# Attention with normalised queries and keys: a warm-up add on GpSimd, another order of the first rows, and last stores behind the join of two branches

## The chip, the cores and the metric

The kernel runs on one core of one Trainium2 chip. Five engines work side by side and meet only through semaphores: TensorE (PE, with its weight loads shown apart as PEld), VectorE (DVE), ScalarE (ACT), GpSimd (POOL) and SyncE (SP), which here only starts transfers. The metric is the device time of one execution in microseconds; less is better. Before the change three executions gave 593.93, 594.44 and 594.76 us, so the median is 594.44 us.

## The reference: what is computed

```python
B, H, S, D = 1, 32, 2048, 640
Dh = D // H                      # 20
# q, k, v: [1, 32, 2048, 20] bfloat16, t: [32] bfloat16
def reference(q, k, v, t):
    eps = 1e-6
    qn = q / (jnp.sqrt((q * q).sum(axis=-1, keepdims=True)) + eps)
    kn = k / (jnp.sqrt((k * k).sum(axis=-1, keepdims=True)) + eps)
    logits = jnp.einsum('bhqd,bhkd->bhqk', qn, kn) * t[None, :, None, None]
    attn = _softmax(logits, axis=-1)
    return jnp.einsum('bhqk,bhkd->bhqd', attn, v)
```

There are 32 heads of 2048 x 2048 logits, with only 20 numbers per row of q and k. The dear part is therefore the exponential of 134 million logits, not the products.

## The kernel before

**Tiling.** Four heads are one group, so there are eight groups; 512 query columns of a group are one block, so there are 32 blocks. In a block each head has 16 key rows of 128 keys. One head's one key row against 512 queries is a unit: 2048 units in all. A unit's logits come from one product of PE (`psA<-qT,kT` or `psD<-qT,kT`, 128 x 512), and the four heads sit in four 32-row strips of PE, since `qpad` and `kpad` hold 20 numbers and 12 zeros for each head.

**Two ways to the exponential.** Two units at a time go through PSUM tile `psA` (two slots) and one ACTIVATE of 128 x 1024 on ACT into `pA`: call this a pair. The other units, taken four heads at a time, go one by one through `psD`: DVE makes an int16 line `dI` of them (a line that, read as float16, is a coarse power of two), and POOL adds a constant to the line twice (`int64_add`, four int16 at once) to give two shifted lines `dS`. These are called D units here. Their sum over four products with `vaug` or `vhalf` is a better exponential than any one of them. So a unit of a pair costs PE one product with v, a D unit four. All products with v add up in one bank of `psD`, with a column of ones in `vaug` giving the softmax's denominator.

**Start.** PE multiplies zeros (`zt`) as a warm-up; `HEAT0` is the count of these. DVE builds the identity `idn`; the first four rows of q and k of group 0 are loaded, squared, summed, rooted on ACT (`nrm`), scaled into `qpad` and `kpad`, turned by PE against `idn` and copied to `qT` and `kT`. The other twelve rows are done on DVE next, k and q, and turned by transposing transfers, except k's rows 4 to 7, which PE turns. POOL fills zeros and makes a band matrix `ind` with two AFFINE_SELECTs.

**The order is planned in Python.** `make_plan` plays the whole kernel through with a cost for each instruction and notes the order for each engine; the chip then runs these orders with semaphore waits. Constants such as `D_FROM` (the share of a block's pairs after which D units may begin), the overhead of a DVE instruction, or `ORDER` (a string that picks one of 23 sets of rules for each stretch of ten pairs) change the order and nothing else. So a small edit to them moves thousands of instructions.

**Two plans.** A flag from t (`flag`, the largest absolute t) picks at run time between a plan that uses D units and one that does not. Every engine loads the flag and branches; each engine's whole program past the first few instructions lies inside the branch's first arm, and the second arm follows it in the program. With the inputs here the first arm runs.

**End.** Each block is drained from `psD` by a transpose on DVE, inverted, and multiplied (`rec`, `omul`) into `ost`. The last block's result leaves in two transfers of 64 partitions, one from SP and one from ACT. They stand as the last instructions of the first arm; then each engine leaves the arm, SP waits for the transfers' landing, and all engines meet in a closing barrier.

The names that the steps below use: `first rows` are in `prep_ops` (called with rows 0 to 4), PE's turning in the loop that fills `pe_pre`, the copies in `copy`, POOL's start in `pool_init`, `sels` and `zeros`, the end in `issue` and `run`.

## Time and profile before

| what | value |
|---|---|
| median of three executions | 594.44 us |
| profiled execution, its own time | 594.49 us |
| span of the profiled execution (first to last instruction) | 592.7 us |
| PE, DVE, ACT, POOL busy | 581.3, 574.6, 580.4, 500.9 us |
| exponentials of 128 x 1024 on ACT | 628 |
| D units (lines `dI` of 128 x 512) | 792 |
| granted TensorE clock, mean | 0.998 |

The busy time of PE counts modelled ends of matmuls that overlap, so it is no sign that PE is full. Busy times of DVE and ACT are reliable as durations from start to written result, but two instructions that follow each other overlap by some ten nanoseconds: the distance from start to start is the better price. A row of the timeline gives start, length, engine, line and operation, the tile that is written and the one that is read, the count of merged instructions, and in brackets the idle time ahead of it and who ended that.

### The profile page before, as it was taken

The numbers are of one execution on the slowest core, as the hardware profiler recorded it, in microseconds if no ns is written. First come the engines' busy times: TensorE is split into PE (matmuls) and PEld (weight loads), VectorE is DVE, ScalarE is ACT, GpSimd is POOL, SyncE is SP. The second block draws the span as 40 slices with busy tenths as digits, with TensorE's granted clock in tenths as the row PEclk, the third lists the DMA queues.
The fourth block names the chain that finished last, engine by engine and source line by source line (L and its number), as shares of the span: only waits on it lengthen the run. The fifth ranks groups of instructions, "written<-read, shape, count | busy, mean of one in ns | idle before, by whom it ended". The sixth has DMA issues, their size and how long they took to land.

```text
span 592.7 us, 16383 instructions
## 1 busy us (share of the span) xinstructions
PE 581.3 (98%) x6768; PEld 160.2 (27%) x6768; DVE 574.6 (97%) x1016; ACT 580.4 (98%) x636; POOL 500.9 (84%) x951
## 2 busy tenths in 40 slices
PE   8999999999999999999999999999999999999996
PEld 4432222322223222232223222222222232222221
DVE  7999999999999999999999999999999999999993
ACT  6999999999999999999999999999999999999995
POOL 2488899878988799887998889987999978999994
PEclk9999999999999999999999999999999999999999
DMA  8700405205051131504033005330406104010000
GB/s 116 108 2 14 104 2 45 47 8 110 3 59 32 31 86 13 79 1 101 19 22 71 1 19 100 24 69 10 92 2 76 32 2 72 2 25 4 7 11 11
DMA packets 132145, 24.20 MB, mean 41 GB/s; under 512 B 121312, under 2 KB 132064, under 8 KB 132064
## 3 DMA queue, kind: packets, MB, share of 16 engines
q1 hardware_dynamic: 131264, 22.96, 24.6%
q8 instruction: 55, 0.90, 0.6%
q14 instruction: 26, 0.21, 0.1%
q10 hardware_dynamic: 800, 0.12, 0.1%
HBM read 7.87 MB, written 2.62 MB: 18 GB/s over the span
## 4 chain that ended last, share of the span: by engine, by line
ACT 87%; PE 10%; DVE 2%; POOL 1%; issue 0%
ACT pA L995 87%; PE psD L815 4%; PE psA L793 3%; PE psA L616 1%; PE psD L612 1%; POOL dS L374 1%; DVE dI L361 0%; PE psD L793 0%; PE psD L749 0%; DVE ssum L294 0%; DVE accT L386 0%; DVE sqs L291 0%; DVE kpad L338 0%; PE psD L616 0%; DVE ost L401 0%
## 5 line engine op out<-in xcount | busy, mean ns | idle before, releaser
L995 ACT ACTIVATE pA<-psA 128x1024 f16<-128x1024 f32 (+1 forms) x628 | 576.2, 1201 | 0.5 <-PE psD L793 0.2
L374 POOL INT64_ADD dS<-dI x935 | 494.5, 545 | 71.3 <-DVE ost L401 14.3
L361 DVE TENSOR_SCALAR dI<-psD 128x512 int16<-128x512 f32 (+1 forms) x768 | 488.1, 695 | 4.3 <-PE psD L793 2.5
L793 PE MATMUL psA<-qT,kT 32*128 32x512 bf16 x1256 | 246.4, 384 | 3.7 <-ACT pA L995 1.0
L793 PE MATMUL psD<-qT,kT 32*128 32x512 bf16 x795 | 237.6, 383 | 0.1
L815 PE MATMUL psD<-dS,vaug 128*22 128x512 f16 x1584 | 201.2, 383 | 0.1
L815 PE MATMUL psD<-pA,vaug 128*22 128x512 f16 (+1 forms) x1256 | 181.1, 383 | 0.3 <-POOL dS L374 0.3
L815 PE MATMUL psD<-dI,vaug 128*22 128x512 f16 x792 | 133.9, 383 | 0.0
L815 PE MATMUL psD<-dI,vhalf 128*22 128x512 f16 x792 | 131.4, 383 | 0.0
L793 PEld LDWEIGHTS psA<-qT,kT 32*128 32x128 bf16 x1256 | 59.0, 90 | 241.1 <-ACT pA L995 235.5
L793 PEld LDWEIGHTS psD<-qT,kT 32*128 32x128 bf16 x795 | 57.3, 91 | 11.1 <-DVE dI L361 4.8
L815 PEld LDWEIGHTS psD<-dS,vaug 128*22 128x22 bf16 x1584 | 42.9, 89 | 58.2 <-issue 38.2
L815 PEld LDWEIGHTS psD<-pA,vaug 128*22 128x22 bf16 x1256 | 39.6, 89 | 49.6 <-issue 41.2
L815 PEld LDWEIGHTS psD<-dI,vhalf 128*22 128x22 bf16 x792 | 29.7, 89 | 27.4 <-issue 20.0
L815 PEld LDWEIGHTS psD<-dI,vaug 128*22 128x22 bf16 x792 | 30.3, 89 | 23.4 <-issue 16.7
L386 DVE STREAM_TRANSPOSE accT<-psD 128x512 f32<-128x512 f32 x32 | 22.6, 705 | 4.6 <-PE psD L815 4.6
L401 DVE TENSOR_TENSOR ost<-accT,rec 128x320 bf16<-128x320 f32 x32 | 17.0, 532 | 0.1
L264 DVE TENSOR_TENSOR sqs<-qk 128x1280 bf16<-128x1280 bf16 x14 | 11.7, 835 | 0.0
L749 PE MATMUL psD<-ind,sqT 128*128 128x128 bf16 x140 | 11.3, 220 | 0.0
L612 PE MATMUL psD<-zt 128*128 128x128 bf16 x123 | 10.3, 221 | 0.0
L749 PEld LDWEIGHTS psD<-ind,sqT 128*128 128x128 bf16 x140 | 7.9, 98 | 4.5 <-issue 3.6
L612 PEld LDWEIGHTS psD<-zt 128*128 128x128 bf16 x123 | 7.0, 98 | 4.9 <-issue 4.9
(59 smaller groups left out, 84.7 us busy)
## 6 DMA issues: line engine op xcount, KB each, us to landing
vaug<-in_v_dram SPq DMA_DIRECT2D x32, 80.0 KB, 4.3
qk<-in_k_dram SPq DMA_DIRECT2D x7, 320.0 KB, 4.0
out_dram<-ost SPq DMA_DIRECT2D x28, 80.0 KB, 1.9
qk<-in_q_dram SPq DMA_DIRECT2D x6, 320.0 KB, 4.3
qk<-in_q_dram SPq DMA_DIRECT2D x4, 80.0 KB, 3.0
out_dram<-ost SPq DMA_DIRECT2D x7, 40.0 KB, 2.1
qk<-in_k_dram SPq DMA_DIRECT2D x1, 240.0 KB, 3.7
qk<-in_q_dram SPq DMA_DIRECT2D x1, 240.0 KB, 4.3
```

What stands on the lines that cost most here:

```text
L264: ops.append(dve("sq", w_, R2, lambda e, o=sq, x=x3: e.tensor_tensor(o, x, x, ALU.mult), [("qk", b, a, i) for i in parts] + [("qkx", b, i) ...
L361: lambda e: e.tensor_scalar(dst, psD[:, pb * QW:(pb + n) * QW], 1024.0 * LOG2E, 15360.0 - 1024.0 * LOG2K + SHIFTS[0], ALU.mult, ALU.add),
L374: lambda e: e.int64_add(o.bitcast(U64), x.bitcast(U64), add), rd, wr)
L386: return dve("drain", QW, R1, lambda e: e.transpose(accT[:, 16 * b:16 * b + 16, :].rearrange("p b d -> p (b d)"), psO_(sb)), [("psD", OB(s ...
L401: dve("omul", 320 * n, R1, lambda e: e.tensor_tensor(dst, num, rcb, ALU.mult), at + ar, [("ost", hg % 2, g) for g in range(g0, g1)]),
L612: return lambda e: e.matmul(bank, zt[:, 0:128], zt[:, 0:n], start=False, stop=False, skip_group_check=True)
L616: o.info = [lambda e: e.matmul(psO[:, :], zt[:, 0:128], zt[:, :])] + [(lambda e, i=i: e.matmul(psA[:, (i % 3) * QW:(i % 3 + 1) * QW], zt[: ...
L749: mms = [lambda e, g=g, j=j: e.matmul(dst, sqT[:, (5 * g + j) * 128:(5 * g + j + 1) * 128], ind[:, j, 96 - 32 * g:224 - 32 * g], start=g + ...
L793: return lambda e: e.matmul(dst, lhsT, rhs, tile_position=(32 * hh, 0))
L815: return lambda e: e.matmul(dst, lhsT, rhs, start=first, stop=last, skip_group_check=True, tile_position=(0, 32 * hh))
L995: a = Op("ACT", "exp", lambda e, s=src, d=dst: e.activation(d, s, ACT.Exp), [("psA", slot)], [("pA", pslot, i) for i in range(WAVES[slot]) ...
```

## The change

1. **GpSimd.** The two AFFINE_SELECTs no longer wait for `kpad`; after them POOL adds zero to a tile of 128 x 4 int16 (`tn`) once with `int64_add`. The zeroing for group 1's tiles moves behind some shifted lines.
2. **First rows.** `first_ops` takes q's and k's first four rows through separate squares, sums, roots and inverses; q is padded first, and k in two halves of two rows. PE's warm-up goes from 18 to 11 products, PE turns q ahead of k, and 3, 3 and 6 short zero products stand between. The copies are shared out anew.
3. **k's rest ahead of q's.** q's twelve remaining rows start only when k's inverse is there (squares) and when k's padded rows are there (sums). `D_FROM` goes from 0.12 to 0.07.
4. **Last stores.** The two last transfers stand behind the join of the two arms. They wait for a semaphore `fin_sem` of their own, which the last `omul` raises.
5. **The plan's numbers.** The overhead that the plan gives a DVE instruction goes from 0.069 to 0.065, a start is noted to the exact time, some other costs change, and `ORDER` is a new string.

```diff
-ORDER = "01i6e8h7238em08g57h5hi2i0gi1j2i0lgea8aa50a567i6538abh965h237050"
+ORDER = "90mfi9dkeb9bb210d6iccig0hgmg2k9baihi0il2h8cjmddh7egj8h9gghegjgc"
-D_FROM = 0.12
+D_FROM = 0.07
-HEAT0 = 18
+HEAT0 = 11
+WARM = (3, 3, 6)
+CPQ = ("DVE", "ACT")
-ACT0 = .0633
+ACT0 = .0634
-TRK = 1.2
+TRK = 0.0
-LOAD1 = 0
+LOAD1 = .12
...
-            o = Op("DVE", name, emit, reads, writes, cost=0.069 + c + ncols_fix,
+            o = Op("DVE", name, emit, reads, writes, cost=0.065 + c + ncols_fix,
...
+        def first_ops():
+            sqf, redf, nrmf, epsf, invf, scf = [], [], [], [], [], []
+            T_ = lambda tl, a: tl[:, a, :, 0:4]
+            for a, pad, nm in ((0, qpad, "qpad"), (1, kpad, "kpad")):
...
+                for c0, c1 in ((0, 4),) if a == 0 else ((0, 2), (2, 4)):
...
+            return sqf + redf + nrmf + [epsf[0]] + invf[0:2] + [scf[0], epsf[1], invf[2]] + scf[1:]
...
-            for o in sels:
+            tune = lambda e: e.int64_add(tn[:, :].bitcast(U64), zt[:, 0:4].bitcast(U64), 0)
+            for o in sels + [Op("POOL", "tune", tune, ["zt", "ind"], ["tn"], 6.0, 6.1)]:
                 o.alone = True
-                o.reads.append(("kpad", 0, 0))
                 want_dve(o, 1)
...
+            pe_pre.extend([warm(WARM[0]), turn("q", 0, 4, [psO, psO, psQ, psQ], [("psD", OB(0)), ("psD", 1)]), warm(WARM[1]),
+                           turn("k", 0, 2, [psD] * 2, [("psD", 0)]), warm(WARM[2])])
+            pe_mid = [turn("k", 2, 4, [psK] * 2, [("psD", 2)])]
...
-            copy("ACT", kT, psD, 0, 128, [("psD", 0)], kk[:1])
-            copy("DVE", qT, psO, 0, 256, [("psD", OB(0))], qq[:2])
-            copy("ACT", qT, psQ, 256, 512, [("psD", 1)], qq[2:])
-            copy("ACT", kT, psD, 128, 512, [("psD", 0)], kk[1:])
+            copy(CPQ[0], qT, psO, 0, 256, [("psD", OB(0))], qq[:2])
+            copy(CPQ[1], qT, psQ, 256, 512, [("psD", 1)], qq[2:])
+            copy("ACT", kT, psD, 0, 256, [("psD", 0)], kk[:2])
+            copy("DVE", kT, psK, 256, 512, [("psD", 2)], kk[2:])
...
                     if o.name == "sq":
-                        o.reads.append(gate)
-                    want_dve(o, 1.5)
+                        o.reads.append(("qT", 0, 1) if a0 else ("rn", 0, (4, 1, 2), 1))
+                    if o.name == "red" and not a0:
+                        o.reads.append(("kpad", 0, R - 1))
+                    want_dve(o, .8 if a0 else .9)
...
+                            if o.name == "omul" and cur == NSB - 1:
+                                o.sem, o.val = fin_sem, 1
...
+                if o.name == "out" and o.sem in ends:
+                    assert o is P.order[e][-1] and [d.sem for d in o.deps] == [fin_sem]
+                    continue
...
                 issue(eng, e, plans[1], cut[e], None)
+            if e == "SP":
+                for x in plans[0][0].order["SP"]:
+                    if x.name == "out" and x.sem not in ends:
+                        eng.wait_ge(x.sem, 16)
+            for o in plans[0][0].order[e][-1:]:
+                if o.name == "out":
+                    eng.wait_ge(fin_sem, 1)
+                    o.emit(eng).then_inc(o.sem, 16)
```

What the edits do to the order of the instructions is seen at three places. The first is PE's start, before (`psA<-zt` of 128 x 512 is the warm-up, `psD<-idn,...` the turning, `psA<-qT,kT` the first logits):

```order
L616 MATMUL psD<-zt 128x512
L616 MATMUL psA<-zt 128x512 x17
L1432 TENSOR_LOAD tmx
L1432 ISA x2
L1433 COMPARE_AND_BRANCH
L624 MATMUL psD<-idn,kpad 128x128 x4
L624 MATMUL psD<-idn,qpad 128x128 x4
L793 MATMUL psA<-qT,kT 128x512 x4
```

and now:

```order
L657 MATMUL psD<-zt 128x512
L657 MATMUL psA<-zt 128x512 x10
L1481 TENSOR_LOAD tmx
L1481 ISA x2
L1482 COMPARE_AND_BRANCH
L675 MATMUL psA<-zt 128x128 x3
L668 MATMUL psD<-idn,qpad 128x128 x4
L675 MATMUL psA<-zt 128x128 x3
L668 MATMUL psD<-idn,kpad 128x128 x2
L675 MATMUL psA<-zt 128x128 x6
L668 MATMUL psD<-idn,kpad 128x128 x2
L840 MATMUL psA<-qT,kT 128x512 x4
```

Seven warm-up products of 512 columns are gone, twelve of 128 columns have come, q is turned first and k in two halves.

The second place is ACT, from its last copy to its end, before (the 1023 exponentials belong to the second arm):

```order
L636 ACTIVATE kT<-psD 128x384
L995 ACTIVATE pA<-psA 128x1024
L1432 TENSOR_LOAD tmx
L1432 ISA x2
L1433 COMPARE_AND_BRANCH
L995 ACTIVATE pA<-psA 128x1024 x627
L458 DMA out_dram<-ost 256x1x80
L1433 UNCONDITIONAL_BRANCH
```

and now:

```order
L685 ACTIVATE kT<-psD 128x256
L1044 ACTIVATE pA<-psA 128x1024
L1481 TENSOR_LOAD tmx
L1481 ISA x2
L1482 COMPARE_AND_BRANCH
L1044 ACTIVATE pA<-psA 128x1024 x625
L1482 UNCONDITIONAL_BRANCH
L1044 ACTIVATE pA<-psA 128x1024 x1023
L1484 UNCONDITIONAL_BRANCH
L491 DMA out_dram<-ost 256x1x80
```

There are 626 exponentials in place of 628, and the last transfer stands behind both arms, so the branch out of the arm comes right after the last exponential.

The third place is POOL between the band matrix and the first shifted lines, before (`ISA` without a tile sets up a library of POOL's; a shifted line is 128x256 in units of four bytes, so 128x512 are two lines):

```order
L546 MEMSET ind 128x5x32
L540 ISA
L540 AFFINE_SELECT ind<-ind 128x5x32 x2
L535 MEMSET kpad 128x64x12
L535 MEMSET qpad 128x64x12
L535 MEMSET vaug 128x64 x2
L1432 TENSOR_LOAD tmx
L1432 ISA x2
L1433 COMPARE_AND_BRANCH
L374 ISA
L374 ISA dS<-dI 128x512 x2
```

and now:

```order
L583 MEMSET ind 128x5x32
L577 ISA
L577 AFFINE_SELECT ind<-ind 128x5x32
L1481 TENSOR_LOAD tmx
L1481 ISA x2
L1482 COMPARE_AND_BRANCH
L577 AFFINE_SELECT ind<-ind 128x5x32
L644 ISA
L644 ISA tn<-zt 128x2
L407 ISA dS<-dI 128x768
```

The library for `int64_add` is now asked for right behind the selects, the zeroing of group 1's tiles no longer stands ahead of it, and the branch comes between the two selects.

Over the whole program the counts of the first arm are: exponentials 628, now 626; D units 792, now 796; `dI` instructions on DVE 744 of 512 and 24 of 1024 columns, now 756 and 20; zero products of PE that fill gaps (128 columns) 123, now 70. Counted along PE's order, the products for D units (`psD<-qT,kT`, a few of them twice) that stand ahead of a given pair are:

| pairs so far | 15 | 20 | 25 | 60 | 100 | 400 | 600 | end |
|---|---|---|---|---|---|---|---|---|
| before | 0 | 6 | 14 | 59 | 115 | 498 | 760 | 795 |
| now | 9 | 15 | 16 | 60 | 115 | 505 | 769 | 798 |

The first of them stands behind the 16th pair before and behind the 9th now; the last behind the 624th of 628 before and behind the 622nd of 626 now. Behind the last pair's logits stood 40 products with v, now 28. PE's first products with a shifted line `dS` stand behind the 21st pair before and behind the 13th now.

110 lines of the change are left out of this document (68 added, 42 removed).

## The prediction

> **What bounds the kernel now.** I read the page's busy times and costliest groups first, then the chain of waits, then one long window of the middle, then the timeline at both ends.
>
> ```profile
> PE 581.3 (98%) x6768; PEld 160.2 (27%) x6768; DVE 574.6 (97%) x1016; ACT 580.4 (98%) x636; POOL 500.9 (84%) x951
> L995 ACT ACTIVATE pA<-psA 128x1024 f16<-128x1024 f32 (+1 forms) x628 | 576.2, 1201 | 0.5 <-PE psD L793 0.2
> L361 DVE TENSOR_SCALAR dI<-psD 128x512 int16<-128x512 f32 (+1 forms) x768 | 488.1, 695 | 4.3 <-PE psD L793 2.5
> 51.27 517.24 ACT pA L995 x564
> 100.00:560.00 460.00, 457.49 (x5383) 121.94 (x5383) 457.16 (x784) 460.00 (x503) 403.11 (x762) 1.00 0.24 40
> ```
>
> The reader is to see that three engines are full at once, which is a balance and not one bound. The exponentials (L995) cover 576.2 us with 0.5 us of idle time among 628: 576.2 / 628 = 0.9175 us each. The chain runs through ACT without a break for 517.24 us. In the window from 100 to 560 us (columns: PE, PEld, DVE, ACT, POOL, clock, DMA share, GB/s) ACT is never idle, and DVE is idle for 460 - 457.16 = 2.84 us only. So the time is made of three pieces that I can price one by one: what lies before the first exponential, 628 exponentials at ACT's pace, and what lies behind the last. Work can be moved from ACT to DVE only as far as DVE has room.
>
> The start:
>
> ```profile
> 3.68 0.49 DVE L291 TENSOR_TENSOR sqs<-qk 128x640 bf16<-128x640 bf16 x1 [0.62 <-DMA qk<-in_q_dram]
> L294 DVE TENSOR_REDUCE ssum<-sqs x5: 486/811/812, 4.3 to 16.9; 128x32 f32<-128x640 bf16 x3, 128x16 f32<-128x320 bf16 x2
> 5.40 0.18 DVE L310 TENSOR_SCALAR rsa<-nr 128x32 f32<-128x32 f32 x1
> 6.00 0.49 DVE L338 TENSOR_TENSOR kpad<-qk,rn 128x320 bf16<-128x320 bf16 x1
> 6.61 0.49 DVE L338 TENSOR_TENSOR qpad<-qk,rn 128x320 bf16<-128x320 bf16 x1
> 1.25 0.61 PE L616 MATMUL psD<-zt 128*128 128x512 bf16 x1 [1.25 <-DVE act_scr L551]
> 1.65 6.38 PE L616 MATMUL psA<-zt 128*128 128x512 bf16 x17
> 6.34 0.15 PEld L616 LDWEIGHTS psA<-zt 128*128 128x128 bf16 x1 [0.28 <-issue]
> 6.77 0.76 PEld L616 LDWEIGHTS psA<-zt 128*128 128x128 bf16 x4 [0.28 <-issue]
> 7.87 0.39 PE L624 MATMUL psD<-idn,kpad 128*128 128x128 bf16 x4
> 8.51 0.42 DVE L639 CAST qT<-psD 128x256 bf16<-128x256 f32 x1 [1.41 <-PE psD L624]
> 9.04 0.40 PE L793 MATMUL psA<-qT,kT 32*128 32x512 bf16 x4 [0.56 <-DVE qT L639]
> 9.47 2.85 ACT L995 ACTIVATE pA<-psA 128x1024 bf16<-128x1024 f32 x3 [0.19 <-PE psA L793]
> ```
>
> Both padded tiles are done at 6.61 + 0.49 = 7.10, but the turning starts only at 7.87, because the warm-up runs to 1.65 + 6.38 = 8.03: the warm-up itself is late.
>
> The end:
>
> ```profile
> 583.86 2.11 ACT L995 ACTIVATE pA<-psA 128x1024 f16<-128x1024 f32 x2
> 586.03 0.81 PE L815 MATMUL psD<-pA,vaug 128*22 128x512 f16 x10
> 587.94 0.49 DVE L401 TENSOR_TENSOR ost<-accT,rec 128x320 bf16<-128x320 f32 x1
> 588.46 0.67 ACTq L458 DMA_DIRECT2D out_dram<-ost  x1
> 588.52 0.53 SPq L458 DMA_DIRECT2D out_dram<-ost  x1
> L1433 ACTq COMPARE_BRANCH  x2: 45/46/47, 10.2 to 589.2; - x2
> L1433 DVEq COMPARE_BRANCH  x2: 51/53/55, 20.8 to 588.0; - x2
> L1439 SPq EVENT_SEMAPHORE  x1: 17/17/17, 590.8 to 590.8; - x1
> L173 DVEq DRAIN  x1: 58/58/58, 590.8 to 590.8; - x1
> L173 SPq DRAIN  x1: 13/13/13, 591.1 to 591.1; - x1
> L173 ACTq DRAIN  x1: 81/81/81, 592.4 to 592.4; - x1
> ```
>
> The last six rows are the engines' sequencers: line, engine, operation, then first and last start. SP has seen both transfers land and drains at 591.1. ACT branches out of its arm at 589.2, behind its transfer, and its first instruction past the join starts at 592.4, 3.2 us later; DVE needs 2.8 us for the same step. The span closes 0.3 us after ACT's drain, so ACT's way out of the arm, not the transfer, ends the kernel.
>
> **The change part by part**, against this execution's own 594.49 us (span 592.7 and 1.8 around it; the median, 594.44, is 0.05 lower).
>
> *Start.* The sum over 640 columns takes 0.81, over 320 it takes 0.49 (the row of L294: median and least of five), so q's part is on its way 0.32 earlier, and k's second square and sum lie beside q's root on ACT. With k's scaling (about half a microsecond from 6.00) no longer ahead, q is padded at about 6.2, and k's two halves by 6.7, in place of 7.10 for both. Warm-up: 11 products at the early spacing of 0.43 (0.15 + 0.28 in the row at 6.34) from 1.25 end near 5.95, three short ones near 6.3. So q turns from 6.45 and is copied from 6.9; k's first half follows, its 256-column copy on ACT goes last, near 7.2 to 7.6. From copy to first exponential it was 9.47 - 8.51 = 0.96; with 0.15 more for k's copy the first exponential falls at 6.9 + 1.11 = 8.05. Gain 9.47 - 8.05 = 1.42. Bounds: 0.6, if PE's spacing has not yet halved (from 0.43 at 6.34 to 0.76 / 4 = 0.19 past 6.77) when the twelve short products and the turning run; 1.7, if k's copy hides. I take 1.4, since q's path ends close to the time at which the spacing halved.
>
> *Two exponentials fewer.* 2 x 0.9175 = 1.84 gained, if the pace holds.
>
> *Four D units more, and room on DVE.* One `dI` line costs 0.60 from start to start:
>
> ```profile
> 68.47 3.67 DVE L361 TENSOR_SCALAR dI<-psD 128x512 int16<-128x512 f32 x6
> ```
>
> (3.67 less one length of 0.68, the median in the row of L361 below, over 5.) Between the 100th and the 600th pair the new order asks 654 D products where the old had 645 (table of the change): 9 x 0.60 = 5.4 us more on DVE in 500 pairs. The window shows 2.84 us idle, so some 2.5 us are lacking at worst, and ACT would wait that long. At best nothing is lost: from pair 20 to the end the new order asks 783 where the old asked 789, because DVE reaches its first D line near 15 us in place of 23.3; and pairs 20 to 100 ask 100 where they had 109, worth up to 0.5 gained there, all the idle time in ACT's row. I take a loss of 0.8, nearer to the good end, because of that balance. q's twelve rows, now queued between D lines, belong to this beginning: their wait for k's padded rows holds nothing that is due before the 25th pair.
>
> *GpSimd.* Setting up a library is the stall here:
>
> ```profile
> L540 POOLq MODIFY_POOL_CONFIG  x2: 11/11/11, 4.2 to 4.3; - x2
> 11.45 0.76 POOL L540 TENSOR_SCALAR_AFFINE_SELECT ind<-ind 128x160 bf16<-128x160 bf16 x2 [7.23 <-DVE rsb L316]
> L374 POOLq MODIFY_POOL_CONFIG  x2: 11/11/11, 19.2 to 19.2; - x2
> 25.35 4.82 POOL L374 INT64_ADD dS<-dI  x10 [6.93 <-DVE dI L361]
> L361 DVE TENSOR_SCALAR dI<-psD x768: 620/680/1225, 23.3 to 581.6; 128x512 int16<-128x512 f32 x182, 128x1024 int16<-128x1024 f32 x10
> ```
>
> From the request at 19.2 to the first add are 6.15 us. The add needs a 128x1024 line that starts at 23.3 and is 1.2 long, done at 24.5, so the last 0.8 was the library's and not DVE's. [...] Now the selects end between 10.3 (set-up counted from k's padding at 6.49, 4.9 us) and 12.6 (as before, plus the branch), the second set-up runs to between 16.5 and 18.9, and the first shifted lines are there by 17.4 to 19.8. PE's first products with `dS` stand behind the 13th pair, whose logits wait for the 11th exponential to leave its slot: 8.05 + 11 x 0.9175 + 0.3 = 18.4. All of PE's later logits are queued behind them. So 0 to 1.4 us lost, once; I take 0.4. Without the added zeros the first real add would pay, later still.
>
> *SP.* k's transposing transfer stood behind group 1's loads and four loads of v; now it is ahead of them:
>
> ```profile
> 17.16 2.05 SPq L446 DMA_TRANSPOSE kT<-kpad  x1
> kT<-kpad SPq DMA_TRANSPOSE x8, 4.4
> ```
>
> k's twelve rows were padded near 14.2 and come 1.4 earlier, 12.8; with the median landing of 4.4 they are there at 17.2, and the 13th pair (26 units, and six D units beside) reaches the ninth row at 18. Cost nothing, with 0.8 us of cover; if the transfer takes longer, PE's queue waits for the difference.
>
> *PE's tail.* Behind the last logits stood 40 products with v, now 28: three rounds of four fewer. The old tail goes from the last exponential's end at 585.97 to PE's end at 586.84; with fewer left over I take 0.3 off, of 0 to 0.6.
>
> *Last stores.* ACT's branch now follows its last exponential, which starts 588.46 - 584.76 = 3.70 us ahead of its store (583.86 + 2.11 - 1.20 = 584.77). The branch's 3.2 us fit in with 0.5 to spare. SP then ends it: its drain at 591.1 is 1.3 ahead of ACT's, and its store can start 0.06 earlier, with ACT's. DVE's drain at 590.8 stays just inside. Nothing but the barrier is queued behind the two new waits. I take 1.4; bounds 0.9 (ACT late by the half microsecond, or DVE next) to 1.5. The rows give 0.046 us for the branch itself and 3.2 to the next instruction. [...]
>
> *Sum*: 594.49 - 1.42 - 1.84 + 0.8 + 0.4 - 0.3 - 1.4 = 590.73, so **590.7 us**, and 590.7 stands for the median too.
>
> **The rivals.**
>
> *DVE becomes the bound.* For it: 2.84 us of idle time against 5.4 us of new work. Against it: in that window DVE was full to 99.4% and ACT never idle. The full 2.5 in place of 0.8 gives 592.4.
>
> *The branch is not hidden, or another engine's takes its place.* If every engine leaves its arm as late as before, the 1.4 stays: 592.1. Against it: the branch stands behind the last exponential in ACT's order; for it, only the half microsecond to spare. [...]
>
> *PE stays at half speed (slower than before).* The warm-up loses seven long products and 53 of the 123 fillers go, and then D units start seven pairs earlier. The spacing halved only after 5.4 us of warm-up (1.25 to about 6.6); 11 products give 4.7 us. [...] At half speed a pair with its D products takes PE 1.7 us (logits, D logits and two rounds of v at 0.43 each) against 0.92 on ACT, so each such pair costs 0.8. It begins with the 9th pair near 15 us; the gain of 3.8 is eaten after five pairs, and eight make it 590.7 + 6.4 = 597.1. Against it: PE is kept busy across the branch by the short products, and a full PE speeds up.
>
> *The plan's edits lose nothing.* With no loss on DVE and POOL: 589.5. This is inside the forecast's own range.
>
> **How the numbers follow.** The forecast with its own range of 589.3 to 591.8 has 0.62, DVE as the bound 0.17, the branch 0.09, half speed 0.05, and 0.07 is left for what the trace does not show. Adding the unknown costs' bounds, the gain runs from 594.49 - 1.7 - 1.84 - 0.5 - 0.6 - 1.5 = 588.4 to 594.49 - 0.6 - 1.84 + 2.5 + 1.4 - 0.9 = 595.1; all at one end is unlikely, so the range is 589.0 to 592.8. What can be told from no change is 0.2%, 1.2 us: faster is below 593.25. The forecast, the branch and most of DVE's case lie below it: 0.90 faster, 0.06 within, 0.04 slower.
>
> **What would show each step.** The first exponential near 8.05, with PE's turning behind q's padding and not behind the warm-up. 626 exponentials covering about 574.4 to 575.5 us; if DVE binds, idle time of ACT over 2 us and DVE idle under 1 us between 100 and 560. POOL's add of zeros ending before 19 and no gap on ACT near 19 to 21. ACT's drain ahead of SP's, SP's drain about 2.6 us behind the store's start. I am wrong if the first exponential is later than 8.9, if ACT's pace passes 0.922, or if an engine's drain still comes more than a microsecond behind SP's.

## The result, and the profile after

The changed kernel takes 589.55 us (median of four executions; three of them lie between 589.43 and 589.59), the kernel before 594.25 us. The ratio is 0.992 with a 95% interval of 0.990 to 0.9939, so about 4.7 us are gained. The fourth execution of the changed kernel took 603.99 us at a mean granted clock of 0.966 and is not in the ratio; no trace of it was kept, and E9 to E11 show how such a time can come about. The profiled execution took 589.51 us with a span of 587.8, against 594.49 and 592.7 before.

The starts of the exponentials in the two traces cut the spans (592.74 and 587.77 us to two digits) into four pieces:

| piece, us | before | after | difference | predicted |
|---|---|---|---|---|
| start to first exponential | 9.47 | 7.77 | -1.70 | -1.42 |
| the next 20 pairs | 18.35 | 19.06 | +0.71 | +0.4 (GpSimd) |
| from there to the last exponential's start | 556.95 | 554.89 | -2.05 | -1.84 + 0.8 |
| last exponential's start to the end | 7.98 | 6.04 | -1.94 | -0.3 - 1.4 |

Together this is -4.98 where -3.76 was predicted. (The expectations below give 19.07 and 0.72 for the second piece, a hundredth more than the starts give.)

Page of the changed kernel: the busy times, and two groups of instructions (busy time, mean ns of one, idle time ahead):

```profile
PE 578.2 (98%) x6731; PEld 159.2 (27%) x6731; DVE 574.9 (98%) x1030; ACT 578.8 (98%) x634; POOL 501.0 (85%) x943
L1044 ACT ACTIVATE pA<-psA 128x1024 f16<-128x1024 f32 (+1 forms) x626 | 574.7, 1194 | 0.9 <-PE psA L840 0.7
L394 DVE TENSOR_SCALAR dI<-psD 128x512 int16<-128x512 f32 (+1 forms) x776 | 489.8, 690 | 2.5 <-PE psD L840 1.5
```

Two windows of it (columns: PE, PEld, DVE, ACT, POOL, clock, DMA share, GB/s), and behind them the second window of the kernel before:

```profile
100.00:560.00 460.00, 457.82 (x5380) 122.93 (x5377) 458.13 (x797) 460.00 (x503) 407.80 (x766) 1.00 0.23 38
8.00:28.00 20.00, 18.57 (x185) 6.98 (x181) 18.84 (x42) 19.78 (x22) 8.19 (x15) 1.00 0.73 92
```

```profile
8.00:28.00 20.00, 19.01 (x216) 9.63 (x213) 17.13 (x37) 19.52 (x24) 5.50 (x12) 1.00 0.93 126
```

The 626 exponentials cover 574.7 us, 574.7 / 626 = 0.918 each: the pace is kept. Between 100 and 560 us ACT is still never idle, while DVE's idle time went from 2.84 to 460 - 458.13 = 1.87 us. So the nine D lines more cost ACT nothing there. What is lost is lost at the beginning: between 8 and 28 us DVE is now busy for 18.84 of 20 us, before for 17.13.

The start in the timeline of the changed kernel:

```profile
1.66 4.47 PE L657 MATMUL psA<-zt 128*128 128x512 bf16 x10
5.62 0.44 DVE L385 TENSOR_TENSOR qpad<-qk,rn 128x320 bf16<-128x320 bf16 x1
6.19 0.39 PE L668 MATMUL psD<-idn,qpad 128*128 128x128 bf16 x4
6.90 0.38 ACT L685 ACTIVATE kT<-psD 128x256 bf16<-128x256 f32 x1
7.34 0.39 PE L840 MATMUL psA<-qT,kT 32*128 32x512 bf16 x4
7.77 4.69 ACT L1044 ACTIVATE pA<-psA 128x1024 bf16<-128x1024 f32 x5 [0.48 <-PE psA L840]
10.90 0.21 DVE L323 SCALAR_TENSOR_TENSOR ssum<-rsa 128x48 f32<-128x48 f32 x1 [0.81 <-DVE rsa L322]
11.66 0.39 PE L862 MATMUL psD<-pA,vaug 128*22 128x512 f16 x3 [0.27 <-DMA vaug<-in_v_dram]
12.64 19.32 ACT L1044 ACTIVATE pA<-psA 128x1024 f16<-128x1024 f32 x20 [0.18 <-PE psA L840]
```

q is padded at 5.62 + 0.44 = 6.06 and turned at 6.19, behind its padding and not behind the warm-up. The 0.81 at 10.09 is DVE's load of the flag with its branch; it now lies in the middle of the chain for k's rows, where nothing hides it.

GpSimd: its sequencer's requests for a library (durations in ns, then first and last start), and behind them its timeline:

```profile
L577 POOLq MODIFY_POOL_CONFIG  x2: 11/11/11, 4.3 to 4.3; - x2
L644 POOLq MODIFY_POOL_CONFIG  x2: 11/11/11, 12.4 to 12.4; - x2
```

```profile
11.40 0.76 POOL L577 TENSOR_SCALAR_AFFINE_SELECT ind<-ind 128x160 bf16<-128x160 bf16 x2 [7.16 <-DVE rsb L324]
18.01 0.18 POOL L644 INT64_ADD tn<-zt  x1 [5.86 <-issue]
18.21 0.83 POOL L407 INT64_ADD dS<-dI  x1
```

The selects start at 11.40 as before (11.45), though they no longer wait for `kpad`: 7.1 us lie between the request at 4.3 and them, as before. The second library was asked for at 12.4 in place of 19.2, and the first shifted line is there at 18.21 + 0.83 = 19.04. PE's first product with it starts at 19.31 without a wait.

The end: the last transfers in the timeline, and behind them the sequencers' rows:

```profile
584.97 0.67 ACTq L491 DMA_DIRECT2D out_dram<-ost  x1
585.03 0.53 SPq L491 DMA_DIRECT2D out_dram<-ost  x1
```

```profile
L1482 ACTq COMPARE_BRANCH  x2: 43/46/49, 8.5 to 581.6; - x2
L1482 DVEq COMPARE_BRANCH  x2: 50/54/57, 10.8 to 584.5; - x2
L175 ACTq DRAIN  x1: 592/592/592, 585.7 to 585.7; - x1
L175 DVEq DRAIN  x1: 58/58/58, 587.4 to 587.4; - x1
L175 SPq DRAIN  x1: 13/13/13, 587.5 to 587.5; - x1
```

ACT leaves its arm at 581.6, 3.3 us ahead of its store, which starts together with SP's, and drains at 585.7. SP is last at 587.5, and DVE, which leaves its arm at 584.5, is only 0.1 us ahead of it.

### The profile page after: what moved, and what is told of

Read it like the earlier page. It is cut to its first block, busy times and chain, and to the rows that moved or that the text cites. A ratio compares the mean times of both kernels' runs of the same rounds, so it can differ in the third digit from the quotient of the medians.

```text
span 587.8 us, 16312 instructions
## 1 busy us (share of the span) xinstructions
PE 578.2 (98%) x6731; PEld 159.2 (27%) x6731; DVE 574.9 (98%) x1030; ACT 578.8 (98%) x634; POOL 501.0 (85%) x943
## 4 chain that ended last, share of the span: by engine, by line
ACT 89%; PE 6%; DVE 4%; issue 0%; DVEq 0%
ACT pA L1044 89%; PE psD L862 3%; PE psA L840 2%; DVE dI L394 2%; PE psA L657 1%; DVE ssum L298 0%; DVE sqs L295 0%; DVE dS L409 0%; DVE rn L326 0%; DVE accT L419 0%; PE psD L657 0%; DVE kT L709 0%; DVEq L1481 0%; DVE kpad L342 0%; DVE qpad L342 0%
## 5 line engine op out<-in xcount | busy, mean ns | idle before, releaser
L1044 ACT ACTIVATE pA<-psA 128x1024 f16<-128x1024 f32 (+1 forms) x626 | 574.7, 1194 | 0.9 <-PE psA L840 0.7
L840 PE MATMUL psD<-qT,kT 32*128 32x512 bf16 x798 | 243.6, 384 | 0.3 <-DVE dI L394 0.2
L862 PE MATMUL psD<-dS,vaug 128*22 128x512 f16 x1592 | 194.2, 383 | 0.4 <-DVE dS L409 0.4
L862 PE MATMUL psD<-pA,vaug 128*22 128x512 f16 (+1 forms) x1252 | 169.0, 383 | 0.4 <-DMA vaug<-in_v_dram 0.3
L862 PE MATMUL psD<-dI,vaug 128*22 128x512 f16 x796 | 130.0, 383 | 0.0
L862 PE MATMUL psD<-dI,vhalf 128*22 128x512 f16 x796 | 125.6, 383 | 0.0
L840 PEld LDWEIGHTS psD<-qT,kT 32*128 32x128 bf16 x798 | 60.1, 91 | 11.3 <-DVE dI L394 4.7
L862 PEld LDWEIGHTS psD<-pA,vaug 128*22 128x22 bf16 x1252 | 37.5, 89 | 46.1 <-issue 39.6
L862 PEld LDWEIGHTS psD<-dI,vhalf 128*22 128x22 bf16 x796 | 28.0, 89 | 28.3 <-issue 19.8
L433 DVE RECIPROCAL rec<-accT 128x16 f32<-128x16 f32 x32 | 7.6, 236 | 0.1
L326 DVE RECIPROCAL rn<-rsa 128x128 f32<-128x128 f32 (+1 forms) x9 | 7.5, 829 | 0.0
```

Of the source, the lines that this page charges most:

```text
L326: add("inv", lambda e: e.reciprocal(rn_, ra), [K("ra")], RN[a0:a1], R1, n * 5 * R1)
L433: dve("rec", 16 * n, R1, lambda e: e.reciprocal(rc, aT[:, :, D]), at, ar, 16 * n * 5 * R1),
L840: return lambda e: e.matmul(dst, lhsT, rhs, tile_position=(32 * hh, 0))
L862: return lambda e: e.matmul(dst, lhsT, rhs, start=first, stop=last, skip_group_check=True, tile_position=(0, 32 * hh))
L1044: a = Op("ACT", "exp", lambda e, s=src, d=dst: e.activation(d, s, ACT.Exp), [("psA", slot)], [("pA", pslot, i) for i in range(WAVES[slot]) ...
```

## The experiments

Each kernel is the changed kernel (or, where it is said, the kernel before) with one edit. Ratios are to the kernel before, so the changed kernel itself stands at 0.992.

**E1 and E2: the last stores, undone and alone.** E1, the changed kernel with the stores in the arm:

```diff
+            outs = [o for o in P.order["SP"] + P.order["ACT"] if o.name == "out"]
...
-                if o.name == "out" and o.sem in ends:
-                    assert o is P.order[e][-1] and [d.sem for d in o.deps] == [fin_sem]
-                    continue
+                if e == "SP" and o.name == "out" and o.sem is ends[0]:
+                    for x in outs:
+                        if x.sem not in ends:
+                            eng.wait_ge(x.sem, 16)
...
-            if e == "SP":
-                for x in plans[0][0].order["SP"]:
-                    if x.name == "out" and x.sem not in ends:
-                        eng.wait_ge(x.sem, 16)
-            for o in plans[0][0].order[e][-1:]:
-                if o.name == "out":
-                    eng.wait_ge(fin_sem, 1)
-                    o.emit(eng).then_inc(o.sem, 16)
```

> The changed kernel with the two last stores back inside the first arm (part 4 of the change undone, all else kept). Theory (the way out of the arm is a fixed price of about 3 us and stands on the path when it follows ACT's store): ACT's store starts near 585.03 as now and ACT's drain 3.9 us behind it, as it was before the change (588.46 to 592.4), so near 589.0; the span is 589.3 in place of 587.8, the time 591.0 (+1.5). Rival (a branch costs its 0.05 us, and the kernel's end moved for another reason, such as the order of the last block): drain near 587.5, time 589.5, no change.

E2 is the kernel before with the reverse edit, `fin_sem` and the two stores behind the join.

> The kernel before with part 4 alone: the last omul raises a semaphore of its own, and both last stores stand behind the join. Theory: the stores start at 588.46 as before, SP's drain 2.56 us behind them near 591.0, ACT's drain ahead of that; span 591.3 in place of 592.7, time 593.1 (-1.4). Rival (the branch stays on the path, or the gain belongs to the new plan): 594.4, no change.

E1 took 591.17 us (ratio 0.9976, 0.9947 to 1.0004), with a span of 589.5, 1.7 above the changed kernel's. Its ACT starts the store at 584.88; the sequencers' rows behind that:

```profile
L1484 ACTq COMPARE_BRANCH  x2: 45/46/47, 8.5 to 585.6; - x2
L175 SPq DRAIN  x1: 13/13/13, 587.5 to 587.5; - x1
L175 ACTq DRAIN  x1: 80/80/80, 589.2 to 589.2; - x1
```

E2 took 592.60 us (0.9976, 0.9966 to 0.9986). Its end:

```profile
L173 ACTq DRAIN  x1: 584/584/584, 588.5 to 588.5; - x1
L173 SPq DRAIN  x1: 13/13/13, 590.3 to 590.3; - x1
```

In E1 SP drains at 587.5, just as in the changed kernel, and ACT 1.7 later: 3.6 us behind its branch, whose own row lasts 0.05. In E2 ACT drains 1.8 ahead of SP. From the last exponential's start (584.11) to the end of the span (590.6) E2 takes 6.5 us where the kernel before takes 8.0. So the way out of the arm is a price of its own, the stores behind the join hide it, and about 1.5 us of gain belongs to this part whatever the plan is.

**E3: no add of zeros.**

```diff
-            tune = lambda e: e.int64_add(tn[:, :].bitcast(U64), zt[:, 0:4].bitcast(U64), 0)
+            tune = lambda e: e.memset(tn[:, :], 0)
```

> The changed kernel with the add of zeros on GpSimd replaced by a plain memset of the same tile (nothing else moves on any engine; the request for the add's library still stands right behind the second select). Theory 1 (the library is loaded from the request on, and the first add only waits for what is left of it): the first shifted line still starts near 18.2, PE's first products with dS near 19.3, time within 0.3 of 589.5. Theory 2, that of the prediction (without the added zeros the first real add pays): three lines dI are there at 18.0, the first shifted line is done 5.6 us later, near 23.8 in place of 19.0, PE's queue stalls for 4 us and ACT with it, less the pairs already in its slots: time 592.5 to 593.5.

589.70 us (0.9928, 0.9916 to 0.9941). GpSimd's timeline:

```profile
18.26 0.83 POOL L407 INT64_ADD dS<-dI  x1 [5.91 <-DVE rsb L324]
```

DVE's third D line, and the requests of GpSimd's sequencer:

```profile
17.35 0.68 DVE L394 TENSOR_SCALAR dI<-psD 128x512 int16<-128x512 f32 x1
```

```profile
L407 POOLq MODIFY_POOL_CONFIG  x2: 11/11/11, 12.5 to 12.6; - x2
```

The first shifted line starts at 18.26 without the add, at 18.21 with it. The releaser in the bracket is an inference: `rsb` was long done. That instruction takes three D lines at once, and the third is done at 17.35 + 0.68 = 18.03, 0.23 us ahead of it. In E5 and E12, where the library had been in use since 18.1 and 18.0 us, the same instruction follows its third D line by the same 0.2. So here DVE's line was most likely the last wait, and the library was up by 18.26 at the latest, 5.8 us behind its request at 12.5, with nothing called in between. The request comes early because the zeroing of group 1's tiles no longer stands ahead of it, and the add of zeros is worth nothing here.

**E4, E5 and E11: the warm-up.** In E4 18 products in place of 11, in E5 4, in E11 11 in the kernel before; the other orders stay:

```diff
-            o.info = [...] + [(...) for i in range(HEAT0 - 1)]
+            o.info = [...] + [(...) for i in range(17)]     # E4; 3 in E5; 10 in E11
```

> The changed kernel with 18 warm-up products of 512 columns as before the change, in place of 11 (no other instruction moves). Theory 1 (the warm-up's end sets the turning, and a later start is lost in full): turning of q near 7.9 in place of 6.19, first exponential 1.4 to 1.7 later, 9.2 to 9.4, time 590.9 to 591.2. Theory 2 (the first 20 pairs took 0.72 us longer than before the change because things tied to other clocks, the fourth load of v and DVE's load of the flag, come late for the earlier start): the same first exponential, but the first 20 pairs take 18.4 to 18.6 us in place of 19.07, and the time is only 0.8 to 1.1 up, 590.3 to 590.6. Rival (the split of the first rows made the gain, the warm-up is no part of it): first exponential near 7.8 and no change.

> The changed kernel with 4 warm-up products of 512 columns in place of 11; nothing else moves. They end near 2.96, and PE then stands idle until q is padded at 6.06. Theory 1 (PE's products go at half speed until it has worked without a break for some time, which in the six traces so far came 2.6 to 6 us after the first product): PE is still at 0.43 per 512 columns at 6.0; the eight products ahead of k's copy take 0.11 each in place of 0.06, so the first exponential falls near 8.3 to 8.5 in place of 7.77, and the halved spacing comes 2.6 to 6 us after 6.0; until then PE keeps up with the pairs (two logits and two products with v, 1.7 us at half speed, against 0.92 on ACT, do not fit once the products with v begin at 10.3), so another 0.5 to 1.5 may be lost: time 590.3 to 591.8. Theory 2 (the change of speed comes at a time of its own, whatever PE does): first exponential near 7.8, time 589.6.

> The kernel before with 11 warm-up products in place of 18, nothing else moved. In the traces so far PE's spacing halved at 3.9 to 7.3 us, and 18 products end between 6.45 and 8.3 by it; q is padded at 6.95 to 7.1. Theory (18 products hold the turning back in the executions in which the spacing halves late, 11 in none): first exponential near 8.4 whatever the spacing, median 593.3 to 593.8 in place of 594.2 to 594.5, and the spread of the executions under 1.2 us in place of 1.8 to 2.3. Rival 1 (the split of the first rows is the whole gain): first exponential as in the kernel before with the same switch, no change. Rival 2 (with 11 products PE is still slow at the turning in many executions): first exponential 8.8 to 9.5, no gain or a loss of up to 0.5.

What came out first was something else: the same instructions take different times. The merged row of the warm-up in the timelines of E2 (its warm-up is that of the kernel before), E4 and E1 (its warm-up is that of the changed kernel):

```profile
1.64 4.96 PE L617 MATMUL psA<-zt 128*128 128x512 bf16 x17
```

```profile
1.66 6.62 PE L657 MATMUL psA<-zt 128*128 128x512 bf16 x17
```

```profile
1.66 3.65 PE L657 MATMUL psA<-zt 128*128 128x512 bf16 x10
```

17 products took 6.38 us before, 4.96 in E2 and 6.62 in E4; ten took 4.47 in the changed kernel and 3.65 in E1. From start to start they are 0.43 apart and then 0.21, and the point of change stands at 3.9 us in E2, 6.06 in the changed kernel, 6.79 in the kernel before and 7.3 in E4. From here on "draw" means this: where the change falls in one execution. The trace's records of the granted clock change at these points, and every distance between two such records of one trace is a multiple of 3.413 us (the record of the full clock lasts 583.68 us in the kernel before and 580.27 in the changed kernel, 171 and 170 times 3.413). So in these traces the clock changes on a grid of 3.413 us, and the grid does not stand still against the kernel's start: its points lie 0.5 us behind the span's start, and multiples of 3.413 further, in E2 and E4, 2.65 in the changed kernel and 3.4 in the kernel before. The change came 2.6 (E2) to 6.0 us (E4) behind the first product at 1.26.

So 18 products end between 6.45 (E2) and 8.13 (E4) by the draw (the start of the last one and one distance more), past q's padding at 6.06 in both, and 11 that are 0.43 apart to the last end at 5.93. They do not always suffice: in E12 the change came at 6.81, the turning began at half speed, and the first exponential fell at 8.13, 0.37 later than in the changed kernel. E4's profiled execution drew the latest point: first exponential at 9.86, 2.1 later than in the changed kernel, and 2.0 of it was still missing at the last exponential (583.73 against 581.72). Its next 20 pairs took 18.97 us against 19.06: theory 2, by which a later start would lose less there, falls. DVE gained no time by the later start: its copy of q stands ahead of its work on k's other rows, and these are scaled from 14.89 on in place of 12.89. Over its executions E4 took 590.51 us (0.9940, 0.9928 to 0.9953), 1.0 above the changed kernel; that lies in theory 2's range, but draws in the middle would give it too, and the trace decides.

E5 shows the other side. Its warm-up ends at 2.9, PE then stands until 6.08, and its clock changes only at 11.48. Two rows of its timeline:

```profile
6.37 0.63 PE L668 MATMUL psD<-idn,qpad 128*128 128x128 bf16 x4
8.97 1.94 ACT L1044 ACTIVATE pA<-psA 128x1024 bf16<-128x1024 f32 x2 [1.01 <-PE psA L840]
```

The turning goes at half speed (0.11 from start to start), and the first exponential is 1.20 later, more than the 0.5 to 0.7 I gave it; 0.28 come back in the next 20 pairs (18.79). 590.45 us (0.9933, 0.9919 to 0.9947): theory 1, at the low end of its time.

E11 gained nothing: 594.56 us (1.0008, 0.9989 to 1.0026). Its first exponential stands at 8.45 in place of 9.47, as the theory had it, but then PE stood in its timeline:

```profile
11.88 0.40 PE L815 MATMUL psD<-pA,vaug 128*22 128x512 bf16 x4 [1.05 <-DMA vaug<-in_v_dram]
```

These products need all four loads of v, and the fourth starts at 7.51 as in the kernel before and lands at 11.84 (with q's last rows loaded behind v, in E8, it lands at 10.51); ACT starts its fifth pair 0.82 us late, at 12.91. In this profiled execution the clock also fell, of which below. In E2, which drew an early change and has its first exponential at 8.40, PE stands at the same place:

```profile
11.54 0.40 PE L816 MATMUL psD<-pA,vaug 128*22 128x512 bf16 x4 [0.76 <-DMA vaug<-in_v_dram]
```

Of its 1.07 us 0.65 are left at the last exponential (584.11 against 584.76). So in the kernel before a good part of an earlier first exponential is lost for lack of v. In the changed kernel the short warm-up is worth about 1.0 us (E4), in the kernel before nothing that shows.

**E6: the old ORDER in the changed kernel.**

```diff
-ORDER = "90mfi9dkeb9bb210d6iccig0hgmg2k9baihi0il2h8cjmddh7egj8h9gghegjgc"
+ORDER = "01i6e8h7238em08g57h5hi2i0gi1j2i0lgea8aa50a567i6538abh965h237050"
```

> The changed kernel with the old ORDER string. The plan then makes 630 exponentials in place of 626 and fewer D units. Theory (ACT's count times its pace, no matter which numbers gave the count): 4 x 0.9175 = 3.7 us more between first and last exponential, time 593.2. Rival (DVE is the bound in the changed kernel, so that fewer D units free DVE and give back what the exponentials cost): time 589.5 to 591.5, and DVE's idle time between 100 and 560 us clearly above the 1.9 us of the changed kernel with ACT's pace below 0.915.

597.70 us (1.0050, 1.0037 to 1.0064), far above both. Its middle window, and a row of its chain of waits (start, length, engine, tile):

```profile
100.00:560.00 460.00, 457.13 (x5326) 122.72 (x5322) 452.09 (x777) 460.00 (x503) 406.74 (x791) 1.00 0.24 39
```

```profile
586.46 4.03 PE psD L862 x72
```

DVE is idle for 7.9 us of the window, and ACT goes no faster: pairs 100 to 600 take 458.45 us against 458.35 in the changed kernel. The rival, DVE as the bound there, falls. But my 3.7 us for four exponentials were less than half of it: the first 100 pairs cost 0.9 more, and behind the last logits stand 72 products with v, where the changed kernel has 28, so that the end takes 9.95 us from the last exponential's start in place of 6.04. A string of ORDER belongs to the numbers it was chosen with; this run tells of the middle, and not what the string alone is worth.

**E7: more work on DVE.**

```diff
+        spare = sbuf("spare", [128, 192], F32)
...
+                    if e == "DVE" and o.name == "drain":
+                        eng.memset(spare[:, :], 0.0)
```

> The changed kernel with one more instruction on DVE behind each of the 32 block drains: a memset of 128 x 192 float32 into a tile that nobody reads, about 0.2 to 0.25 us each by the rows of the other memsets (0.27 for 128 x 256), so 6 to 8 us of DVE work in all, some 6 of it between 100 and 560 us. The added output is not used. Theory 1 (DVE's room is its idle time of 1.87 us between 100 and 560, and beyond it each microsecond on DVE is one on ACT): 4 to 6 us longer, time 593.5 to 595.5, with ACT idle in the page's groups of exponentials. Theory 2 (DVE still has slack that its busy time hides, since its lines are buffered and the 9 lines more of the changed order cost nothing): less than 1.5 us longer, time below 591.

590.83 us (0.9937, 0.9924 to 0.9951), 1.3 above the changed kernel. DVE's timeline of E7, and then the same place in the changed kernel:

```profile
302.53 0.71 DVE L420 STREAM_TRANSPOSE accT<-psD 128x512 f32<-128x512 f32 x1
303.23 0.22 DVE L1479 MEMSET spare<- 128x192 f32 x1
303.37 3.01 DVE L395 TENSOR_SCALAR dI<-psD 128x512 int16<-128x512 f32 x5
```

```profile
302.04 0.71 DVE L419 STREAM_TRANSPOSE accT<-psD 128x512 f32<-128x512 f32 x1
302.67 3.08 DVE L394 TENSOR_SCALAR dI<-psD 128x512 int16<-128x512 f32 x5
```

From the drain's start to the next line's are 0.84 us in place of 0.63, here and as the median of all 32 drains, so each memset costs DVE 0.21, or 6.7 us for 32. ACT paid 1.0 of it between its first and its last exponential. Nor did DVE's idle time pay: it fell by 1.18 us (1.87 to 0.69). The lines themselves paid: five of them take 3.01 in place of 3.08, from start to start 0.58 in place of 0.60, and over the window the mean distance behind a line of 512 is 0.605 before the change, 0.603 after it and 0.596 in E7. A D line that waits a few hundredths for PE starts within the length of the one ahead (0.68 long, 0.60 apart), so the profile counts no idle time. This overlap is more than the ten nanoseconds or so that I gave ahead of the change: 0.08 us for D lines, and 0.28 for exponentials (1.19 long, 0.918 apart). Theory 2 holds: DVE has room that neither its busy nor its idle time shows.

**E8, E9, E10 and E12: where the first 20 pairs lose 0.71.** E8 loads q's last rows behind v. E9 moves DVE's branch behind the scaling of k's rows and q's squares and sums behind that. E10 has both. E12 also puts the first two D lines ahead of q's second sum. As moves in an order (SP's, then DVE's), with the plan's names: `ldq`, `ldv` are loads, `sq` and `red` squares and sums of q's rows, `rs0` to `rt` the small steps of a root and inverse, `nmk` the scaling of k's rows, `cp` the copy kT<-psD, `P1` a D line:

```diff
-ldq ldv ldv ldv ldv
+ldv ldv ldv ldv ldq                    # E8, E10, E12
-rs2 [branch] rs3 rs4 eps inv rt sq nmk sq red cp red rs0 rs1 P1 rs2 P1
+rs2 rs3 rs4 eps inv rt nmk [branch] sq sq cp red red rs0 rs1 P1 rs2 P1    # E9, E10
+rs2 rs3 rs4 eps inv rt nmk [branch] sq sq cp red P1 P1 red rs0 rs1 rs2    # E12
```

> The changed kernel with the load of q's last twelve rows of group 0 issued on SP behind the four loads of v in place of ahead of them (only SP's order changes). PE waited 0.27 us for the fourth load of v at 11.66, and ACT's largest early gap is 0.30 at 11.43. Theory (the first 20 pairs take 0.72 longer than before the change partly because of this load): the wait is gone, the gap with it, the first 20 pairs take 18.7 to 18.8 in place of 19.07, the span is 0.25 to 0.35 shorter, time 589.2. Rival 1 (the gap only moves to the next late thing, DVE's chain for k's rows, which loads the flag in its midst): 19.0, no change. Rival 2 (q's rows come too late, needed at 12.5): a new wait of DVE near 12.5 and a time up to 1 us longer.

> The changed kernel with DVE's load of the flag and its branch moved behind the scaling of k's twelve rows (they stood in the midst of that chain, 0.81 us without work at 10.09), and with q's squares and sums that stood ahead of that scaling and of the copy kT<-psD behind them. Theory (in the first 20 pairs PE's queue stands at the turning of k's rows 4 to 7, which waits for this chain): kpad is written at 11.7 to 12.4 in place of 12.9 to 13.5, the copy kT<-psD starts near 14.0 in place of 14.43, the gaps of ACT at 13.62 and 16.51 (0.16 and 0.12) go, that at 11.43 (0.30, the fourth load of v) stays; first 20 pairs 18.7 to 18.85 in place of 19.07, span 0.2 to 0.35 shorter, time 589.3. Rival (the later sums of q delay the D units that DVE begins at 15.88, and the loss comes back there): 19.0 to 19.2, no change.

> The same with the load of q's last rows behind the loads of v as well (the two edits that alone only move the gap). Theory: neither wait is left, the gaps of ACT up to the 20th pair are below 0.1 each, first 20 pairs 18.3 to 18.5 as before the change (18.35), span 587.1 to 587.3, time 588.9 to 589.1. Rival (a third late thing takes the place, such as the copy of k's rows 4 to 7 or the waits of D logits for dI): 18.7 to 19.0, time 589.4.

> The two edits before (the flag behind k's scaling, q's last rows loaded behind v) and one more: DVE's first two D lines stand ahead of the second sum of q's last rows and of the three small steps behind it, not behind them. In the two runs before, PE stood 0.60 us at its third D product, waiting for dI, and the granted clock fell to a half at the end of the 3.4 us in which that wait lay (18.3 and 17.8 us). Theory: the wait is gone, and with it both the third gap of ACT (0.53 at 17.39) and the fall of the clock, so the clock is 0.997 or more in every execution; first 20 pairs 18.3 to 18.5, span 587.1 to 587.3, time 588.8 to 589.2. Rival (what brings the clock down is the small share of work that the products with 32 rows and 22 columns are, with fewer filling products between, and not one wait): the profile or other executions still show a clock of 0.975 to 0.995 and times of 591 to 600.

E8: 589.84 us (0.9918, 0.9905 to 0.9932), no change. Rows of its timeline:

```profile
7.82 6.52 ACT L1044 ACTIVATE pA<-psA 128x1024 bf16<-128x1024 f32 x7 [0.48 <-PE psA L840]
13.65 0.40 PE L668 MATMUL psD<-idn,kpad 128*128 128x128 bf16 x4 [0.57 <-DVE kpad L342]
14.73 5.70 ACT L1044 ACTIVATE pA<-psA 128x1024 f16<-128x1024 f32 x6 [0.39 <-PE psA L840]
```

The wait for v is gone and ACT runs seven pairs without a gap; then PE stands 0.57 us at the turning of k's rows 4 to 7, and 20 pairs take 19.11 us. This is rival 1. E10 takes that wait away too, and PE stands at the third D product, 0.60 us at 16.48, waiting for `dI`. E12 takes this one away, and in its timeline PE stands later still:

```profile
8.13 11.11 ACT L1044 ACTIVATE pA<-psA 128x1024 bf16<-128x1024 f32 x12 [0.48 <-PE psA L840]
18.56 0.39 PE L840 MATMUL psD<-qT,kT 32*128 32x512 bf16 x1 [0.68 <-DVE dI L394]
19.69 12.79 ACT L1044 ACTIVATE pA<-psA 128x1024 f16<-128x1024 f32 x13 [0.45 <-PE psD L840]
```

Twelve pairs without a gap, then 0.67 us at once, and 20 pairs take 19.20 us; 590.32 us (0.9940, 0.9927 to 0.9954). Each edit took away the wait that it was aimed at. In E8 and E12 the loss, 0.76 and 0.85 us, was back before the 20th pair, behind something else that DVE had not yet done; in the traces of E9 and E10 PE slows down ahead of that pair, so their 20 pairs cannot be compared. This fits a DVE that has too much to do between 8 and 28 us (18.84 of 20 us in the changed kernel, 19.03 in E12), whatever the order. E5 fits it too: its third pair starts at 11.23, 1.6 us later than in the changed kernel, while DVE scales k's rows only 0.88 later (13.77 against 12.89), and the 18 pairs from there take 16.52 us, 0.918 each, without a loss. The loads of v had more time there as well, so E5 does not tell the two apart. It is shown that none of these waits is the cause by itself; that the sum of DVE's work there is, is argued, since no run took work from it. No version here beats the changed kernel by more than the noise.

E9 (592.32 us; 0.9966, 0.9942 to 0.9991) and E10 (591.03; 0.9945, 0.9927 to 0.9964) cannot be read by their times. In their profiled executions PE falls back to half speed, and other executions of theirs with a mean clock of 0.975 to 0.994 point to the same. Windows of E10 (the column behind the five engines is the granted clock):

```profile
10.00:14.00 4.00, 4.00 (x42) 1.89 (x41) 3.47 (x10) 4.00 (x5) 0.98 (x2) 1.00 0.34 77
14.00:18.00 4.00, 3.40 (x35) 1.47 (x33) 3.90 (x12) 3.68 (x5) 0.00 (x0) 0.97 1.15 197
18.00:44.00 26.00, 26.00 (x166) 5.23 (x164) 17.70 (x28) 18.39 (x19) 13.12 (x23) 0.50 0.44 57
```

From 17.8 to 45.1 us the clock is 0.50 and ACT is busy for 18.39 of 26 us: it waits for PE's logits, and some 7.6 us are lost. In E9 this lasts from 18.3 to 49.1 us, in E11 from 13.8 to 30.9; the three stretches are 8, 9 and 5 times 3.413 us. In each case the fall comes at a point of the grid behind a stretch in which PE stood, for 0.60 us in E9 and E10 and 1.05 in E11. But such a stand does not always bring it: the 0.76 us of E2 did not, nor did E12's own 0.68 us at 18.56, to which E12 only moved the stand. E12's profile shows no fall, while two of its five executions (591.3 us) have a mean clock of 0.994 against 0.999 in the others. So E12's theory falls, and its rival's signs are there; that these two executions had a fall is likely and not traced. PE's rows cover 2.82 of the 3.41 us ahead of the fall in E9 and in E10, but only 2.45 of an earlier stretch in E9 that had no such end, so a share of busy time does not decide it either. What does stays open.

## Why the prediction was right, and where a term was not

The time, 589.55 us, lies within the range (589.0 to 592.8) and the forecast's own (589.3 to 591.8), 1.15 us below the 590.7. About 1.0 of this is one term, the room on DVE; of the other misses those of the start and of the first 20 pairs cancel, which is luck.

- **Start**, -1.42: measured -1.70, its upper bound, but not for the reason I had given for that bound. PE's turning comes behind q's padding, as forecast. From q's copy to the first exponential it was 7.77 - 6.62 = 1.15, where I had 1.11: k's copy does not hide. The copy itself starts at 6.62 and not at 6.9, since PE was at full speed from 6.06 on; in E12, where it was not until 6.81, the copy starts at 6.99. What the step did not see is that the 8.03 at which the old warm-up ended was one draw. With E2's draw the same step would have been worth 8.40 - 7.77 = 0.63, the lower bound, which I had given for another reason.
- **Two exponentials**, -1.84: the pace of 0.918 held, and in E6 it is no quicker with 6 us less on DVE.
- **Room on DVE**, +0.8: this is the step that failed. It took the window's 2.84 us of idle time for all the room there was, so that 5.4 us of new lines had to cost up to 2.5. From the 20th pair to the last exponential the change gained 2.05, 0.2 more than the two exponentials; the term is about -0.2 there. E7 shows why: 6.7 us more on DVE cost ACT 1.0. The lower bound, "pairs 20 to 100 ask fewer", was nearer, but for the wrong reason: pairs 20 to 100 took 73.63 us against 73.56.
- **GpSimd**, +0.4: the place was right, the engine wrong. The second library was up at 18.0 and PE did not wait for a shifted line. The loss of 0.71 in these pairs is, by E8 to E12, most likely DVE's: the rival "DVE becomes the bound" then came true for 20 pairs and not for 600. That the first real add would pay without the added zeros fell with E3: the library was up without a call.
- **k's transfer ahead**, 0: right, no wait for it is in the trace, though k's rows are padded at 12.89 + 0.65 = 13.54 and not at 12.8, with DVE's load of the flag, 0.81 us, in their chain.
- **PE's tail**, -0.3: the drain starts 1.68 us behind the last exponential's start in place of 2.14, -0.46, within its 0 to 0.6.
- **Last stores**, -1.4: -1.48 from the last drain's start to the end, and E1 and E2 give 1.7 and 1.5. The step is shown from both sides. ACT's way out took no more than the 3.3 us that it had. DVE's drain was just inside as forecast, by 0.1 us, so nothing more is to be had here without DVE's branch. The branch's own row lasts 0.05, and the way to the next instruction is another thing: 3.0 us from DVE's branch to its drain, 3.6 from ACT's in E1. In the trace of the kernel before, four packets of the DMA queues that the page calls `instruction` (q8 and q14) start between 590.38 and 591.37 us, between ACT's branch at 589.2 and its drain at 592.4; that ACT waited for one of these is a guess and not shown, as the trace does not tell whose they are.
- **PE at half speed**: the rival that I gave 0.05 did not happen in the executions compared, and yet it is real. Its place near 15 us and its size were near: the traces of E9, E10 and E11 have the fall between 13.8 and 18.3 us and lose some 6 to 11 us by it. The mechanism was another. I had PE stay at half speed for want of long products; in all three traces it had reached full speed, between 4.1 and 7.0 us, and fell back. E11, which keeps the old fillers and the late D units, falls too. I also had the "either or" wrong: it is a draw of each execution. By their mean clocks one of the four executions of the changed kernel (0.966) and three of the twelve of E1 (0.983 to 0.985, 597.1 to 598.0 us, which widen its interval) had it, and none of the 68 of the kernel before that ran beside the experiments (0.996 or more). So the gain of 4.7 us is that of an execution without a fall.

## What to carry to other kernels

An engine's idle time was not its room here: DVE was idle for 1.87 us, and 6.7 us more of work on it cost ACT 1.0 (E7). Its D lines start 0.08 us within the tail of the one ahead, so a wait as small as that is counted as busy, and only a dose of extra work tells what the engine can still take. When taking away a wait moves the loss to the next late instruction of the same engine, the order is not the cause; count that engine's work in the stretch as the next suspect. What an engine does behind its last work can have a price of microseconds (3.0 to 3.6 for leaving the branch here), and with the last transfers behind it the kernel ended 1.5 (E2) to 1.7 us (E1) sooner. And a warm-up is judged over several executions, since the point at which PE speeds up was a draw of 3.4 us here (3.9 in E2, 7.3 in E4); the single executions are to be looked at too, since a median of four does not show that one of them is 14 us longer.

## What the runs showed of the hardware that I had not expected

- The granted clock of TensorE changed on a grid of 3.413 us whose points lie elsewhere against the kernel's start from trace to trace (0.5, 2.65 and 3.4 us behind it). Under an unbroken warm-up from 1.26 us the change came at 3.90 us in one trace (E2) and at 7.30 in another (E4). In both of these the stretch of the grid that ends near 3.9 us had PE at work for 2.64 and 2.63 us; the clock rose at its end in the one and not in the other.
- PE fell back to half speed (a granted clock of 0.50) in three traces, each time behind a stand of 0.60 (E9, E10) to 1.05 us (E11), while stands of 0.68 (E12) and 0.76 us (E2) in two others brought no fall. It needed 17.1 (E11) to 30.8 us (E9) to come back, though PE was busy for 16.00 of 16 us (E11) and 26.00 of 26 (E10) in between.
- The first instruction of a library of GpSimd started 5.6 us (the add, 12.4 to 18.0) to 7.1 us (the selects, 4.3 to 11.4) behind the request in the changed kernel. In E3, where nothing was called between the request and the first real add, that add started 5.8 us behind the request (12.5 to 18.26).
- D lines of 128 x 512, 0.68 us long, start 0.60 apart, and 0.58 apart in E7, where DVE has been given more to do.
